# Block-sparse attention with a low-rank mixer: scores of two heads on the row halves of TensorE, a 0/1 mask product, and a searched instruction order

## The chip, the cores and the metric

One core of one Trainium2 chip. The metric is the device time of one execution in microseconds (us), the median of several runs. Every run has a state (fast or slow). Engines are called by the names in the profile: PE is TensorE's matmul row, PEld its weight loads, DVE is VectorE, ACT is ScalarE, POOL is GpSimd, and SPq is the queue of SyncE, which asks for most of the transfers (DMA: copies between the chip's memory and the core's tiles). In the profile's lines `est<-ps` means that tile est is written from tile ps; the tiles qld, kld and vld are where loads of queries, keys and values land.

## The reference, cut to what matters

Four batches, eight heads, 768 positions, 64 channels per head. Attention with a mask of 24 x 24 blocks of 32 positions: a window, the first and last block row and column, and three sampled blocks per row. Then a mixer: u = x + low-rank product over positions, and u + relu(u W1) W2 with 512 and 2048 channels.

```python
scores = scale * np.matmul(q, k.transpose(0, 1, 3, 2))        # 768 x 768 per head
scores = np.where(mask, scores, -1000000000.0)                # mask from sampled_blocks
attn = np.exp(scores - max) ; attn = attn / sum
x = np.matmul(attn, v)                                        # heads side by side: (4, 768, 512)
h = x.transpose(0, 2, 1) @ U @ V                              # rank 32
u = x + h.transpose(0, 2, 1)
out = u + np.maximum(u @ w_ch1, 0.0) @ w_ch2                  # 512 -> 2048 -> 512
```

## The kernel before: the parts that the argument touches

The work goes by pairs of heads: 16 pairs, four per batch (pair 0 to 3 are batch 0). The mask is in the scores themselves. Queries and keys lie in a tile with 64 data rows and 24 more rows of the 128 (block numbers as one-hot, and a bias of 0 or -240), so that one 128-row matmul gives score plus bias, and exp makes the masked entries vanish.

```python
def scores(i, h, g):                       # pair i, head h, block of 128 keys g
    qT, kT = augs[i]                       # 64 data rows + 24 mask rows
    psc = pscp.tile([P, 2, 512], FP32, tag="psc", name="psc")     # two PSUM banks
    for c in range(2):
        nc.tensor.matmul(psc[:, c, 0:HS], kT[:, h, g * P : (g + 1) * P],
                         qT[:, h, c * HS : (c + 1) * HS], start=True, stop=True)   # 384 columns
    nc.scalar.activation(out=est[:, g]..., in_=psc[:, :, 0:HS], func=AF.Exp, scale=0.125)
...
def av(self, h, g):                        # value product: 6 matmuls of 65 columns
...
def w1(jj, c):                             # first MLP product: 4 matmuls of 384 columns, then a ReLU
def w2(sc, part):                          # second MLP product: 4 matmuls of 512 columns
...
if i + 2 < NPAIR:
    with behind:
        last = load_qk(i + 2)              # SyncE: queries, keys
        load_v(i + 2)                      # SyncE: values
    with tc.issue_after(last.ins):
        if i == 0: load_w1((0, 1))
        elif i == 1: load_w1((2, 3))
        elif i == 4: load_w2((0, 4))       # half of the second product's weights
        elif i == 5: load_w2((8, 12))      # the other half
```

The kernel uses PSUM, where TensorE writes its results, as eight banks of 512 float32 columns. Here pools hand them out as they come free: four for scores, one for the value product, three for the rest.

The softmax here doesn't subtract the row's maximum and nothing guards it: scores larger than these inputs give would overflow.

Of the kernel before, what the change touches and what calls it, by code (L numbers as in the profile page):

```python
# [16 lines left out]
P = 128  # L17
# [3 lines left out]
def kernel(  # L21
# [29 lines left out]
    NST = 2  # L51
# [14 lines left out]
    oh_np = np.zeros((P, T, D), dtype=np.float16)  # L66
    oh_np[cols % P, cols // P, blk] = 1.0

# [11 lines left out]
    oh_dr = nc.inline_tensor(oh_np, name="onehot_const")  # L80
# [6 lines left out]
    epool = ctx.enter_context(tc.tile_pool(name="epool", bufs=2))  # L87
    xpool = ctx.enter_context(tc.tile_pool(name="xpool", bufs=2))
    upool = ctx.enter_context(tc.tile_pool(name="upool", bufs=2))
    tpool = ctx.enter_context(tc.tile_pool(name="tpool", bufs=18))  # L90
# [3 lines left out]
    pscp = ctx.enter_context(  # L94
        tc.tile_pool(name="pscp", bufs=2, space=bass.MemoryType.PSUM)
    )
    psvp = ctx.enter_context(
        tc.tile_pool(name="psvp", bufs=1, space=bass.MemoryType.PSUM)
    )
    psmp = ctx.enter_context(  # L100
        tc.tile_pool(name="psmp", bufs=3, space=bass.MemoryType.PSUM)
    )

    def psm(shape, dtype):
        return psmp.tile(shape, dtype, tag="pm", name="pm")

    id16 = consts.tile([P, P], FP16)
    oh = consts.tile([P, T, D], FP16)
# [6 lines left out]
    qst = [consts.tile([P, 2, T, P], FP16, name=f"qst{i}") for i in range(NST)]  # L115


# [4 lines left out]
    kst = [consts.tile([P, 2, T, P], FP16, name=f"kst{i}") for i in range(NST)]  # L122
# [7 lines left out]
    def load_qk(i):  # L130
        b, hp = divmod(i, HP)
        last = None
        for src, st, nm in ((q, qst, "qld"), (k, kst, "kld")):
            ld = ldpool.tile([P, 2, T, D], FP32, tag="ld" + nm, name=nm)
            nc.sync.dma_start(
                out=ld,
                in_=src[b, 2 * hp : 2 * hp + 2].rearrange("h (p t) d -> p h t d", t=T),
            )
            if i < NPE:
                sts[i, nm] = stpool.tile([P, T, 2, D], FP16, tag="st" + nm, name="st" + nm)  # L140
                dst = sts[i, nm].rearrange("p t h d -> p h t d")
            else:
                dst = st[i % NST][:, :, :, 0:D]
            last = nc.gpsimd.tensor_copy(out=dst, in_=ld)  # L144
        return last
# [45 lines left out]
    def first_turn(h, n, c):  # L191

        if n == 1:
            pt = psm([P, HS], FP32)
        elif c == 0:
            pt = pw[:, 1, 0:HS]
        else:
            pt = pscp.tile([P, 2, 512], FP32, tag="psc", name="psc")[:, 0, 0:HS]
# [9 lines left out]
    with tc.manual_schedule(  # L208
# [5 lines left out]
        pw = pscp.tile([P, 2, 512], FP32, tag="psc", name="psc")  # L214
# [7 lines left out]
        pks = [psvp.tile([P, HS], FP32, tag="pv", name="pv"), psm([P, HS], FP32)]  # L222
# [78 lines left out]
    def mask_columns():  # L301
        def both(ap):
            return ap[:, None].broadcast_to([P, 2, T, D])

        nc.sync.dma_start(out=oh, in_=oh_dr.ap())
        pb = psm([P, T, D], FP32)
        for t in range(T):
            nc.tensor.matmul(
                pb[:, t, :], ohT[:, t * P : (t + 1) * P], bias[0:NB, 0],
                start=True, stop=True,  # L310
            )
        nc.vector.tensor_copy(out=kst[0][:, 0, :, D:], in_=pb)
        nc.gpsimd.tensor_copy(out=kst[0][:, 1, :, D:], in_=kst[0][:, 0, :, D:])
        for i in range(NST):
            nc.gpsimd.tensor_copy(out=qst[i][:, :, :, D:], in_=both(oh))
            if i > 0:
                nc.gpsimd.tensor_copy(out=kst[i][:, :, :, D:], in_=kst[0][:, :, :, D:])

# [28 lines left out]

    def front(i):
        augs[i] = (qres[i % 2], kres[i % 2])
        for st, aug in zip((qst, kst), augs[i]):  # L350
            last = nc.sync.dma_start_transpose(
                aug.rearrange("d h (t p) -> d (h t) p", t=T),
                st[i % NST].rearrange("p h t d -> p (h t d)"),
            )
        return last
# [21 lines left out]
    ests = {}  # L377

    def scores(i, h, g):
        qT, kT = augs[i]  # L380
        if g == 0:
            ests[h] = epool.tile([P, T, S], FP16, tag="est", name="est")
        est = ests[h]
        psc = pscp.tile([P, 2, 512], FP32, tag="psc", name="psc")
        for c in range(2):
            nc.tensor.matmul(  # L386
                psc[:, c, 0:HS],
# [5 lines left out]
            out=est[:, g].rearrange("k (c n) -> k c n", c=2), in_=psc[:, :, 0:HS],  # L393
            func=AF.Exp, scale=0.125,
        )
        return est

    class Batch:
        def __init__(self):
            self.xf = xpool.tile([P, T, HD], FP32, tag="xf", name="xf", bufs=3)  # L400
# [5 lines left out]
            self.tT = []  # L406


    class Pair:
        def __init__(self, i, bt):  # L410
            self.b, self.hp = divmod(i, HP)
            self.bt = bt
            self.ests = {}
            self.pu = {}
            self.xh = xpool.tile([P, T, P], FP16, tag="xh", name="xh", bufs=3)
            self.ch = slice(self.hp * P, (self.hp + 1) * P)
            self.xbar = NPE <= i < NPAIR - 1

        def av(self, h, g):

            head = 2 * self.hp + h
            if g == 0:
                self.pav = psvp.tile([P, T, D + 1], FP32, tag="pv", name="pv")
            pav, est = self.pav, self.ests[h]
            for sc in range(T):
                nc.tensor.matmul(  # L426
                    pav[:, sc, :],
                    est[:, g, sc * P : (sc + 1) * P],
                    vts[self.b % 2][:, head, g, 0 : D + 1],
                    start=(g == 0 and sc == 0), stop=(g == T - 1),  # L430
                    skip_group_check=True,
                )
            if g == T - 1:
                rcp = misc.tile([P, T], FP32, tag="rcp", name="rcp")
                nc.vector.reciprocal(out=rcp, in_=pav[:, :, D])  # L435
                for dst in (
                    self.xh[:, :, h * D : (h + 1) * D],
                    self.bt.xf[:, :, head * D : (head + 1) * D],
                ):
                    self.last = nc.vector.tensor_tensor(  # L440
                        out=dst, in0=pav[:, :, 0:D],
                        in1=rcp[:, :, None].broadcast_to([P, T, D]), op=ALU.mult,
                    )

        def mix(self):
            pa = psm([P, P], FP32)
# [5 lines left out]
            nc.vector.tensor_copy(out=self.bt.a16[:, self.ch], in_=pa)  # L452


        def ut_x(self, c):
            pu = self.pu[c] = psm([P, HS], FP32)
            for j in range(3):
                nc.tensor.matmul(
                    pu[:, j * P : (j + 1) * P], self.xh[:, 3 * c + j, :], id16,
# [3 lines left out]
        def ut_a(self, c):  # L463
# [6 lines left out]
            nc.vector.tensor_copy(  # L470
                out=self.bt.uT[self.hp][:, c * HS : (c + 1) * HS], in_=self.pu[c]
            )


        def add(self, c):
            if c == 0:
                self.u16 = xpool.tile([P, T, P], FP16, tag="u16", name="u16")
            pu = psm([P, 3, P], FP32)
# [7 lines left out]
            nc.vector.tensor_add(out=self.u16[:, ts, :], in0=self.xh[:, ts, :], in1=pu)  # L486
            nc.vector.tensor_add(out=xf, in0=xf, in1=pu)  # L487
            if c == 1 and self.xbar:
                nc.sync.dma_start_transpose(
                    self.bt.uT[self.hp].rearrange("c (t p) -> c t p", t=T),  # L490
                    self.u16.rearrange("p t c -> p (t c)"),
                )

        def turn(self):
            pt = psm([P, S], FP16)
# [4 lines left out]
            nc.vector.tensor_copy(out=self.bt.uT[self.hp], in_=pt)  # L500


    def mlp_steps(b, bt):
        def w1(jj, c):
            if c == 0:
                bt.tT.append(tpool.tile([P, S], FP16, tag="tT", name="tT"))
            pt = psm([P, HS], FP32)
            for cc in range(NCC):
                nc.tensor.matmul(  # L509
                    pt,  # L510
                    w1t[:, cc, jj * P : (jj + 1) * P],
                    bt.uT[cc][:, c * HS : (c + 1) * HS],
                    start=(cc == 0), stop=(cc == NCC - 1),
                )
            dst = bt.tT[jj][:, c * HS : (c + 1) * HS]
            if c == 0:
# [4 lines left out]
        hold = {}  # L521

        def w2(sc, part):
            if part == 0:
                hold[sc] = psm([P, HD], FP32)
                if b == 0:
                    nc.tensor.matmul(  # L527
                        hold[sc], Vt[:, sc, :], bt.a16, start=True, stop=False
                    )
            for jj in range(4 * part, 4 * part + 4):  # L530
                nc.tensor.matmul(  # L531
                    hold[sc],
                    bt.tT[jj][:, sc * P : (sc + 1) * P],
                    w2t[:, jj, :],
                    start=(b > 0 and jj == 0), stop=(jj == NJJ - 1),
                )
            if part == 3:
                of = opool.tile([P, HD], FP32, tag="of", name="of")
                nc.vector.tensor_add(out=of, in0=bt.xf[:, sc, :], in1=hold[sc])  # L539
# [4 lines left out]
        def last_half(c):  # L544
# [184 lines left out]
```

## Time and profile before

| | before |
|---|---|
| time, median (runs made beside the changed kernel) | 298.88 us |
| span of the profiled run | 296.7 us |
| first to last matmul start | 292.1 us |
| of that, explained by the columns streamed | 284.2 us |
| unexplained, first 20 us / later | 4.7 / 3.3 us |

The page of the profile: busy time of an engine with its share of the span, the busy share in 40 slices as tenths, the granted TensorE clock as tenths, and the chain of work that ended last.

```profile
PE 291.4 (98%) x2775; PEld 182.3 (61%) x2775; DVE 142.0 (48%) x299; ACT 179.8 (61%) x261; POOL 50.2 (17%) x70
PE   8999999999999999999999999999999999999995
PEclk9999999999999999999999999999999999999999
...
PE 87%; ACT 12%; issue 0%; DVE 0%
...
L392 ACT ACTIVATE est<-psc 128x768 f16<-128x768 f32 x192 | 149.6, 812 | 51.6 <-PE psc L386 50.7
L386 PE MATMUL psc<-qres,kres 128*128 128x384 f16 x384 | 93.5, 325 | 1.0 <-ACT est L392 0.7
```

A group's line ends with its busy time, the mean ns of one, and its engine's idle time before it. The 325 ns of a matmul is its recorded length, and such records overlap. What counts in a stream is the time from one start to the next, and the trace gives that too: 162.8 ns behind 384 columns, 215.8 ns behind 512 and 109.2 ns behind 256. That agrees with the formula of the Trainium skill, "TensorE: Matmul & The Clock Gate", section "Back-to-back issue gap": columns divided by 2.4 plus 2.5 ns. The section calls this the gap of an isolated matmul, though, and says that a sustained stream takes some 131 ns for 512 columns; this trace has 215.8 ns in the stream, so I go by the formula. The 65-column value products start some 30 ns apart. I call a start-to-start time *explained* as far as this formula goes (at least 29.5 ns). The rest is *unexplained*: a wait, a slow clock, or a change of row tiling. The sums of explained and unexplained time in this document are worked out in this way from the matmul starts in the trace.

So from 60 us on TensorE is a full stream, and a column less is time less. Before about 41 us, exps of batch 0 on ScalarE set the pace.

One more reading matters. Six small matmuls at 32.5 us use 24 rows of the array, and the others 128. From the timeline (start, time in us, engine, line, and "xN" merged):

```profile
32.04 0.48 PE L386 MATMUL psc<-qres,kres 128*128 128x384 f16 x2
32.46 0.34 PE L308 MATMUL pm<-bias,small 24*128 24x64 f16 x6
32.74 0.35 PE L426 MATMUL pv<-vt,est 128*128 128x65 f16 x6
```

The second score matmul started at 32.204 us and streams for 163 ns; the first of 24 rows starts only at 32.459, 92 ns late. The way back costs 92 ns again.

### The profile page before, as it was taken

Reading aid. Unit: us, or ns where it says so; the run is one execution under the profiler, and the core shown is the slowest. Engines: PE = TensorE matmul, PEld = TensorE weight load, DVE = VectorE, ACT = ScalarE, POOL = GpSimd, SP = SyncE. Lnnn points to the kernel's source line nnn. Section 1 sums busy time; section 2 is a strip of 40 time slices with the busy share of each in tenths; the row PEclk is TensorE's granted clock in tenths of the full one; section 3 lists DMA queues with packets and bytes.
Section 4 is the critical chain, followed back from the end, with each engine's and each line's share of the span. In section 5 each row is a group of like instructions: output and inputs, shape, how many; then the busy total and the mean of one; then the engine's idle time right before and its main releaser. Section 6 shows DMA issues by size and latency. Waiting matters only on the chain.

```text
span 296.7 us, 6622 instructions
## 1 busy us (share of the span) xinstructions
PE 291.4 (98%) x2775; PEld 182.3 (61%) x2775; DVE 142.0 (48%) x299; ACT 179.8 (61%) x261; POOL 50.2 (17%) x70
## 2 busy tenths in 40 slices
PE   8999999999999999999999999999999999999995
PEld 3677776666666555666665556666665655565444
DVE  7766776346452525454452624346462535443112
ACT  5999997587766655767775555777875530332000
POOL 4773184014031212030201203030000000000000
PEclk9999999999999999999999999999999999999999
DMA  6899949096959494744719385662510121000111
GB/s 192 288 315 235 295 154 144 8 254 94 170 187 231 136 225 139 163 139 72 224 29 240 121 178 198 141 188 43 92 29 35 39 62 73 36 0 2 71 71 71
DMA packets 58661, 39.94 MB, mean 135 GB/s; under 512 B 40152, under 2 KB 55144, under 8 KB 58632
## 3 DMA queue, kind: packets, MB, share of 16 engines
q1 hardware_dynamic: 55764, 35.19, 43.9%
q0 software_dynamic: 2688, 4.19, 8.3%
q8 instruction: 21, 0.34, 0.5%
q10 hardware_dynamic: 180, 0.15, 0.1%
q14 instruction: 8, 0.07, 0.1%
HBM read 27.72 MB, written 6.29 MB: 115 GB/s over the span
## 4 chain that ended last, share of the span: by engine, by line
PE 87%; ACT 12%; issue 0%; DVE 0%
PE pm L509 28%; PE pm L531 27%; PE psc L386 16%; ACT est L392 12%; PE pv L426 9%; PE pm L448 1%; PE psc L218 1%; PE pm L481 1%; PE pm L550 1%; PE pm L527 0%; PE pm L497 0%; PE pm L364 0%; PE pm L201 0%; PE psc L201 0%; DVE of L555 0%
## 5 line engine op out<-in xcount | busy, mean ns | idle before, releaser
L392 ACT ACTIVATE est<-psc 128x768 f16<-128x768 f32 x192 | 149.6, 812 | 51.6 <-PE psc L386 50.7
L509 PE MATMUL pm<-uT,w1t 128*128 128x384 f16 x512 | 94.6, 326 | 0.0
L386 PE MATMUL psc<-qres,kres 128*128 128x384 f16 x384 | 93.5, 325 | 1.0 <-ACT est L392 0.7
L531 PE MATMUL pm<-w2t,tT 128*128 128x512 f16 x368 | 90.7, 379 | 0.0
L509 PEld LDWEIGHTS <-w1t 128*128 128x128 f16 x512 | 47.1, 98 | 27.0 <-issue 0.2
L426 PEld LDWEIGHTS <-est 128*128 128x128 f16 x1152 | 51.9, 97 | 16.5
L519 DVE TENSOR_SCALAR tT<-pm 128x384 f16<-128x384 f32 x64 | 35.6, 556 | 51.3 <-PE pm L509 48.6
L426 PE MATMUL pv<-vt,est 128*128 128x65 f16 x1152 | 55.7, 193 | 0.0
L517 ACT ACTIVATE tT<-pm 128x384 f16<-128x384 f32 x64 | 31.4, 490 | 38.2 <-PE pm L509 25.5
L386 PEld LDWEIGHTS <-kres 128*128 128x128 f16 x384 | 36.0, 97 | 27.0 <-issue 1.9
L531 PEld LDWEIGHTS <-tT 128*128 128x128 f16 x368 | 33.3, 98 | 30.1
L144 POOL CAST qst<-qld 128x768 f16<-128x768 f32 x10 | 8.3, 827 | 120.5 <-DMA qld<-in_q_dram 120.5
L539 DVE TENSOR_TENSOR of<-xf,pm 128x512 f32<-128x512 f32 x23 | 15.7, 684 | 25.9 <-PE pm L531 25.9
L435 DVE RECIPROCAL rcp<-pv 128x6 f32<-128x6 f32 x32 | 6.1, 192 | 38.1 <-PE pv L426 38.1
L440 DVE TENSOR_TENSOR xh<-pv,rcp 128x384 f16<-128x384 f32 x32 | 17.8, 557 | 1.0
L486 DVE TENSOR_TENSOR u<-xh,pm 128x384 f16<-128x384 f16 x24 | 13.2, 551 | 9.8 <-PE pm L481 9.3
L440 DVE TENSOR_TENSOR xf<-pv,rcp 128x384 f32<-128x384 f32 x32 | 17.5, 547 | 0.0
L154 POOL CAST vt<-vld 128x768 f16<-128x768 f32 x16 | 13.3, 828 | 14.7 <-DMA vld<-in_v_dram 14.2
L487 DVE TENSOR_TENSOR xf<-xf,pm 128x384 f32<-128x384 f32 x24 | 13.1, 547 | 0.0
L452 DVE CAST a<-pm 128x128 f16<-128x128 f32 x16 | 4.7, 291 | 15.9 <-PE pm L448 15.8
L144 POOL CAST kst<-kld 128x768 f16<-128x768 f32 x10 | 8.3, 827 | 5.1 <-DMA kld<-in_k_dram 5.1
L448 PE MATMUL pm<-xh,Ut 128*128 128x128 f16 x96 | 8.0, 219 | 0.0
(75 smaller groups left out, 111.2 us busy)
## 6 DMA issues: line engine op xcount, KB each, us to landing
vld<-in_v_dram SPq DMA_DIRECT2D x16, 384.0 KB, 5.3
out_dram<-of SPq DMA_DIRECT2D x23, 256.0 KB, 2.0
qld<-in_q_dram SPq DMA_DIRECT2D x15, 384.0 KB, 4.6
kld<-in_k_dram SPq DMA_DIRECT2D x15, 384.0 KB, 5.0
w1t<-in_moe_w_ch_dram POOLq DMA_DIRECT2D x4, 512.0 KB, 10.6
w2t<-in_moe_w_ch_dram POOLq DMA_DIRECT2D x4, 512.0 KB, 6.3
qld<-in_q_dram SPq DMA_DIRECT2D x2, 192.0 KB, 3.3
kld<-in_k_dram SPq DMA_DIRECT2D x2, 192.0 KB, 3.3
```

Source lines behind the costliest of these rows:

```text
L144: last = nc.gpsimd.tensor_copy(out=dst, in_=ld)
L154: nc.gpsimd.tensor_copy(out=vts[b % 2][:, 2 * hp : 2 * hp + 2, :, 0:D], in_=ld)
L386: nc.tensor.matmul(psc[:, c, 0:HS], kT[:, h, g * P : (g + 1) * P], qT[:, h, c * HS : (c + 1) * HS], start=True, stop=True,)
L392: nc.scalar.activation(out=est[:, g].rearrange("k (c n) -> k c n", c=2), in_=psc[:, :, 0:HS], func=AF.Exp, scale=0.125,)
L426: nc.tensor.matmul(pav[:, sc, :], est[:, g, sc * P : (sc + 1) * P], vts[self.b % 2][:, head, g, 0 : D + 1], start=(g == 0 and sc == 0), st ...
L440: self.last = nc.vector.tensor_tensor(out=dst, in0=pav[:, :, 0:D], in1=rcp[:, :, None].broadcast_to([P, T, D]), op=ALU.mult,)
L486: nc.vector.tensor_add(out=self.u16[:, ts, :], in0=self.xh[:, ts, :], in1=pu)
L509: nc.tensor.matmul(pt, w1t[:, cc, jj * P : (jj + 1) * P], bt.uT[cc][:, c * HS : (c + 1) * HS], start=(cc == 0), stop=(cc == NCC - 1),)
L517: nc.scalar.activation(out=dst, in_=pt, func=AF.Relu)
L519: nc.vector.tensor_scalar_max(out=dst, in0=pt, scalar1=0.0)
L531: nc.tensor.matmul(hold[sc], bt.tT[jj][:, sc * P : (sc + 1) * P], w2t[:, jj, :], start=(b > 0 and jj == 0), stop=(jj == NJJ - 1),)
L539: nc.vector.tensor_add(out=of, in0=bt.xf[:, sc, :], in1=hold[sc])
```

## The change

Intent: in the scores of batches 1 to 3 only 64 of the 128 rows carry data, so two heads can run at once, head 0 on rows 0 to 63 and head 1 on rows 64 to 127. The mask rows no longer fit. The mask becomes a 0/1 tile, multiplied onto the exps by VectorE. The order of TensorE, VectorE and ScalarE and the PSUM bank of each product come from a list found by a search.

```diff
-    pscp = ctx.enter_context(tc.tile_pool(name="pscp", bufs=2, space=bass.MemoryType.PSUM))
-    psvp, psmp = ...                                   # (cut)
+    PS = psum.tile([P, 8, 512], FP32, name="ps")       # all eight banks; the list names the bank
...
+    PLAN = """
+    S e S K7 e K2 k S k A A e S v R7 e S t M2 e S m R6 e S t A5 A e S A A e S X7 A e S A A6 e S
+    ...                                                # 848 entries, cut
+    p Q D6 e e W d W p W V6 p f Q v V7 e e U6 v p U5 a U3 a p U7 a U6 a Q a M6 e e U7 m U6 b p
+    """                # Q double step, H half step, e exp, p mask product, U W MLP, a b ReLU on ACT/DVE
...
+    def half_quad(i, j, hs):                           # key blocks 2j, 2j+1 of the heads hs
+        for h in hs:
+            units[h] = PS[:, 3 * h : 3 * h + 3, :].rearrange("p b n -> p (b n)")   # 3 banks a head
+        for u, lo, hi in ((0, 0, 512), (0, 512, S), (1, 0, 256), (1, 256, S)):
+            g = 2 * j + u
+            for h in hs:
+                nc.tensor.matmul(units[h][:, u * S + lo : u * S + hi],
+                    kT[drows[h], g * P : (g + 1) * P], qT[drows[h], lo:hi], ...)   # 64 rows
+        for h in hs:
+            exp of 128x1536 on ScalarE; then
+            nc.vector.tensor_mul(out=both[h], in0=both[h], in1=mask[:, 2 * j : 2 * j + 2, :])
...
+    def mask_tile():                                   # in batch 0, once
+        for r in range(16):
+            for d in range(3):
+                ts = [t for t in range(T) if (6 * r + t) // BLK == d]
+                if ts:
+                    nc.sync.dma_start(out=mask[r : P : 16, ts[0] : ts[-1] + 1, :],
+                        in_=table[8 * d : 8 * d + 8, None, :].broadcast_to([8, len(ts), S]))
```

There are 34 double steps and 4 half steps. The mask tile takes 18 transfers on SyncE.

## The prediction

> **What bounds the kernel.** TensorE's stream of columns. In the trace a matmul starts after the one before it by a time that grows with the columns of the one before: 162.8 ns for 384 columns, 215.8 ns for 512, some 30 ns for the 65-column value product. Summed over all matmuls these times make 284.2 of the 292.1 us from first to last matmul; of the 7.9 us left, 4.7 lie in the first 20 us and 1.8 in the next 20. From 60 us on TensorE loses 0.1 us in each 20. The chain of waits agrees: PE 87%, ACT 12% (exps of batch 0, to about 41 us). After that VectorE (48% busy) and ScalarE (61%) have slack.
>
> **What it removes.** Scores of pairs 4 to 15 are now 64 rows deep. They were 288 matmuls of 384 columns (46.8 us). Now 34 double steps have four matmuls per head (512, 256, 256, 512 columns), the heads on opposite row halves. Side by side, a step streams 650 ns plus some 30 ns offset instead of 1300: 23.1 us for 34. Four half steps have one head alone and gain nothing (2.6 us). Saved: about 21 us. The skill page "TensorE: Matmul & The Clock Gate", Part 3, says matmuls on different row groups run concurrently; nothing in this trace shows it yet.
>
> **What it adds.**
> - Changing the row tiling drains the array ("TensorEngine Tiling (Array Packing)", Key Properties). The trace agrees: around the six 24-row matmuls at 32.5 us the stream stops 92 ns on entry and 92 on leaving. 38 steps times two: 7 us.
> - VectorE: 72 mask products of 128x1536 f16. The trace has no such form. My estimate is 0.9 us each at two elements per cycle (65 us in all), 1.7 us at one. ReLUs move away: 64 to 39 on VectorE (556 ns each, -14 us), 64 to 89 on ScalarE (490 ns). VectorE then has about 145 us of work in the 235 us after batch 0.
> - ScalarE: 72 exps of 1536 columns for 144 of 768 (702 ns start to start); estimated 1.34 us each.
> - PSUM: a double step holds six of eight banks until two exps, 2.7 us, are over. Meanwhile the MLP has two banks and what comes free. There new stalls of TensorE can arise; the order was searched to avoid them. I allow 2 us.
> - DMA: 1.2 MB of mask rows while the first pairs load, half as much transposing later. Off the path.
>
> **The sum.** 298.95 - 21 + 7 + 2 - 2 (some of the early waits) = 285 us. All of it counts, because TensorE's stream is the path. Batch 0, to about 45 us, should hardly change.
>
> Prediction: 284.5 us, range 277 to 293. Chances: faster by over 2% 0.84, within 2% 0.11, slower 0.05.
>
> **What would show each step.** In the timeline the heads' score matmuls start some 30 ns apart, and a step takes about 0.7 us. The gaps before and after a step are about 90 ns longer than the columns explain. Mask products last 0.9 us. TensorE's unexplained time after 60 us sums to about 7 us plus stalls. ScalarE and VectorE stay under 75% busy; the chain stays mostly PE.
>
> **What would make it wrong.** No concurrency of the halves (then about 306 us). Weight loads of a half that aren't hidden behind its own matmul (some 60 ns each, 10 us in all). Mask products at one element per cycle: VectorE would hold back value products and MLP banks, several us. A cheaper drain: down to 279. PSUM stalls above 2 us.

## The result, and the profile after

The changed kernel takes 332.44 us (332.27 to 333.10, four runs) against 298.88 us: **11.2% slower**, ratio 1.112, 95% interval 1.110 to 1.114. Ratios in this document are the mean time of one kernel's fast runs over that of the other's of the same rounds, so not quite the ratio of the medians that are quoted.

The same parts of the page, changed kernel (L568 is the first MLP product, L722 the row-half scores, L731 their exps, L737 the mask product):

```profile
PE 285.3 (86%) x2759; PEld 166.3 (50%) x2759; DVE 192.7 (58%) x342; ACT 182.0 (55%) x214; POOL 51.1 (15%) x66
PE   6899904996689889898789999988979899999995
PEclk9999965999599999999999999999999999999999
...
PE 57%; DMA 16%; ACT 13%; SPq 6%; issue 5%; POOL 2%; DVE 1%; POOLq 0%; ACTq 0%
...
L731 ACT ACTIVATE est<-ps 128x1536 f16<-128x1536 f32 x72 | 100.7, 1448 | 48.1 <-PE ps L722 47.3
L737 DVE TENSOR_TENSOR est<-est,mask 128x1536 f16<-128x1536 f16 x72 | 72.0, 1002 | 22.5 <-ACT est L731 22.5
L722 PE MATMUL ps<-qpl,kpl 64*128 64x512 f16 (+1 forms) x288 | 31.9, 328 | 0.0
```

PE has holes now: the sixth and seventh slice (41 to 58 us), the tenth and eleventh (74 to 91 us), with the clock down to 5 or 6 tenths in three of these, and many slices at 8. Only 57% of the chain is PE now, where it was 87%; transfers, exps and SyncE's queue have 35%. VectorE, at 58%, is not crowded.

The row halves themselves did what they should. These are the starts (ns from the first) of the eight score matmuls of the double step at 138.86 us, with their columns:

```
0 (512)   3 (512)   226 (256)   230 (256)   336 (256)   339 (256)   445 (512)   448 (512)
```

Two heads start 3 ns apart and a step streams 664 ns (median of 34), where two heads one after the other would take about 1300.

Who waited for whom on TensorE (us in total, times, longest), changed kernel:

```profile
PE ps L568 <- ACT est L731: 13.1, 15, 1.1
PE ps L672 <- POOL stqld L149: 12.6, 1, 12.6
PE ps L595 <- DMA w2t<-in_moe_w_ch_dram: 6.1, 2, 4.3
PE ps L500 <- ACT est L731: 3.7, 4, 1.0
PE ps L288 <- DVE kres L240: 1.6, 1, 1.6
PE ps L568 <- DMA uT<-u: 1.5, 1, 1.5
PE ps L534 <- ACT est L731: 0.8, 1, 0.8
```

The balance of TensorE from first to last matmul start, in us. "Stop" is an unexplained time over 0.45 us. The last column is the best kernel of the experiments, further down:

| | before | changed | e7 |
|---|---|---|---|
| columns | 284.2 | 262.1 | 263.8 |
| changes between row tilings | 0.2 | 7.1 | 8.0 |
| unexplained, first 20 us | 4.7 | 6.5 | 5.3 |
| stops after 20 us | 0 | 41.9 | 2.6 |
| the rest (small waits, slow clock) | 3.1 | 8.4 | 4.2 |
| first to last matmul | 292.1 | 326.1 | 283.9 |

The columns fell by 22.1 us and the changes of tiling cost 7.1: as predicted. The 41.9 us of stops were not. They are of four kinds:

1. **12.8 us at 41.5 us**: TensorE wants to turn the queries of pair 5, and they have not arrived. Timelines of SyncE's queue and of GpSimd, first before:

```profile
20.75 0.37 SPq L135 DMA_DIRECT2D qld<-in_q_dram  x1
```

and in the changed kernel:

```profile
19.82 28.26 SPq L664 DMA_DIRECT2D mask<-table  x18
48.18 1.35 SPq L144 DMA_DIRECT2D qld<-in_q_dram  x1
...
53.61 0.83 POOL L149 CAST stqld<-qld 128x768 f16<-128x768 f32 x1 [17.47 <-DMA qld<-in_q_dram]
```

The 18 mask transfers take SyncE's queue from 19.8 to 48.2 us. The queries of pair 5, asked for at 20.75 us before, are asked for at 48.18 us, and GpSimd casts them at 53.6. The queue's own waits say that part of the 28 us is waiting for earlier transfers:

```profile
SPq L664 <- DMA kld<-in_k_dram: 5.1, 1, 5.1
SPq L664 <- DMA qld<-in_q_dram: 3.3, 1, 3.3
SPq L664 <- DMA vld<-in_v_dram: 2.5, 1, 2.5
```

   Each issue in the trace carries one of eight semaphores in turn. From the third mask issue on, an issue also waits on that semaphore, which the transfer eight before it had used. The quickest issues take 0.60 us, others 1.44 us, one 1.60 us (16.7 us for all 18; the rest of the 28 us is nearly all waiting); why, these runs don't settle.

2. **4.5 and 2.1 us at 79.5 and 85.4 us**: the second half of the weights of the second MLP product has not landed. Its two transfers land at 84.11 and 87.70 us, and TensorE goes on at 84.15 and 87.74.

3. **20.9 us in 20 stops of 0.6 to 1.3 us**: a product placed after a double step waits for the step's second exp. One of them, timelines of TensorE and ScalarE (L595 is the second MLP product, L500 the mixer):

```profile
133.70 0.82 PE L722 MATMUL ps<-qpl,kpl 64*128 64x512 f16 x8
134.45 1.04 PE L595 MATMUL ps<-w2t,tT 128*128 128x512 f16 x4
135.33 0.38 PE L588 MATMUL ps<-a,Vt 128*128 128x512 f16 x1
135.54 1.03 PE L595 MATMUL ps<-w2t,tT 128*128 128x512 f16 x4
137.40 0.49 PE L500 MATMUL ps<-xh,Ut 128*128 128x128 f16 x6 [0.83 <-ACT est L731]
...
134.56 2.79 ACT L731 ACTIVATE est<-ps 128x1536 f16<-128x1536 f32 x2 [1.37 <-PE ps L722]
```

   The two exps end at 137.35 us. L500 is written into bank 5, which the second of them was reading (the list says "M5"), and starts at 137.40.

4. **1.7 us at 149.7 us** for a transposed u.

After a long stop the clock is low, too. From the view by stretches (span of the stretch, busy times, granted clock, DMA share, GB/s), changed kernel:

```profile
41.00:60.00 19.00, 6.34 (x74) 4.67 (x72) 4.09 (x11) 3.72 (x5) 4.08 (x6) 0.64 0.63 155
79.00:92.00 13.00, 6.95 (x54) 3.74 (x54) 3.73 (x7) 2.79 (x2) 1.70 (x3) 0.61 0.62 101
```

"TensorE: Matmul & The Clock Gate", Part 1, says that TensorE's clock falls to half after an idle window of about 3.4 us and comes back after a busy one. The trace agrees in part. Behind the 4.5 us stop 512-column matmuls start 427 ns apart instead of 216, and the two stretches of half clock last 13.65 and 10.24 us, four and three times 3.41. But the clock fell already 2.7 and 2.3 us into the two longest stops, before 3.4 us of idling had passed.

### The profile page after: what moved, and what is told of

Same layout as the page of the kernel before. It is cut to its first block, busy times and chain, and to the rows that moved or that the text cites. A ratio compares the mean times of both kernels' runs of the same rounds, so it can differ in the third digit from the quotient of the medians.

```text
span 330.5 us, 6605 instructions
## 1 busy us (share of the span) xinstructions
PE 285.3 (86%) x2759; PEld 166.3 (50%) x2759; DVE 192.7 (58%) x342; ACT 182.0 (55%) x214; POOL 51.1 (15%) x66
## 4 chain that ended last, share of the span: by engine, by line
PE 57%; DMA 16%; ACT 13%; SPq 6%; issue 5%; POOL 2%; DVE 1%; POOLq 0%; ACTq 0%
PE ps L568 22%; PE ps L595 18%; ACT est L731 13%; PE ps L722 8%; DMA vld<-in_v_dram 8%; PE ps L406 5%; SPq L664 4%; DMA w2t<-in_moe_w_ch_dram 2%; DMA uT<-u 2%; DMA qld<-in_q_dram 2%; PE ps L500 1%; DMA vld<-in_moe_V_dram 1%; PE ps L534 1%; DMA kld<-in_k_dram 1%; PE ps L615 1%
## 5 line engine op out<-in xcount | busy, mean ns | idle before, releaser
L731 ACT ACTIVATE est<-ps 128x1536 f16<-128x1536 f32 x72 | 100.7, 1448 | 48.1 <-PE ps L722 47.3
L568 PE MATMUL ps<-uT,w1t 128*128 128x384 f16 x512 | 95.7, 326 | 14.7 <-ACT est L731 13.1
L595 PE MATMUL ps<-w2t,tT 128*128 128x512 f16 x368 | 91.0, 384 | 6.1 <-DMA w2t<-in_moe_w_ch_dram 6.1
L737 DVE TENSOR_TENSOR est<-est,mask 128x1536 f16<-128x1536 f16 x72 | 72.0, 1002 | 22.5 <-ACT est L731 22.5
L578 ACT ACTIVATE tT<-ps 128x384 f16<-128x384 f32 x89 | 43.7, 491 | 70.4 <-PE ps L568 69.4
L568 PEld LDWEIGHTS <-w1t 128*128 128x128 f16 x512 | 47.9, 97 | 52.1 <-issue 22.5
L595 PEld LDWEIGHTS <-tT 128*128 128x128 f16 x368 | 34.9, 99 | 44.8 <-issue 11.0
L406 PE MATMUL ps<-vt,est 128*128 128x65 f16 x1152 | 45.3, 196 | 0.0
L580 DVE TENSOR_SCALAR tT<-ps 128x384 f16<-128x384 f32 x39 | 21.6, 555 | 29.6 <-PE ps L568 29.3
L706 ACT ACTIVATE est<-ps 128x768 f16<-128x768 f32 x36 | 26.2, 810 | 13.3 <-PE ps L697 13.3
L722 PE MATMUL ps<-qpl,kpl 64*128 64x512 f16 (+1 forms) x288 | 31.9, 328 | 0.0
L603 DVE TENSOR_TENSOR of<-xf,ps 128x512 f32<-128x512 f32 x23 | 15.7, 683 | 27.3 <-PE ps L595 27.3
L722 PEld LDWEIGHTS <-kpl 64*128 64x128 f16 x288 | 11.8, 95 | 16.1 <-issue 10.7
L474 DVE TENSOR_TENSOR xh<-ps,rcp 128x384 f16<-128x384 f32 x32 | 17.8, 558 | 1.1
L161 POOL CAST vt<-vld 128x768 f16<-128x768 f32 x16 | 15.0, 936 | 11.2 <-DMA vld<-in_v_dram 10.2
L469 DVE RECIPROCAL rcp<-ps 128x6 f32<-128x6 f32 x32 | 6.2, 193 | 17.6 <-PE ps L406 17.6
```

What stands on the lines that cost most here:

```text
L406: nc.tensor.matmul(pav[:, sc, :], est[:, n, sc * P : (sc + 1) * P], vts[b % 2][:, 2 * hp + h, g, 0 : D + 1], start=(g == 0 and sc == 0), s ...
L474: self.last = nc.vector.tensor_tensor(out=dst, in0=pav[:, :, 0:D], in1=rcp[:, :, None].broadcast_to([P, T, D]), op=ALU.mult,)
L568: nc.tensor.matmul(pt, w1t[:, cc, jj * P : (jj + 1) * P], bts[b].uT[cc][:, c * HS : (c + 1) * HS], start=(cc == 0), stop=(cc == NCC - 1),)
L578: nc.scalar.activation(out=dst, in_=pt, func=AF.Relu)
L580: nc.vector.tensor_scalar_max(out=dst, in0=pt, scalar1=0.0)
L595: nc.tensor.matmul(po, tts[b, c, jj][:, s * P : (s + 1) * P], w2t[:, jj, :], start=(b > 0 and jj == 0), stop=(jj == NJJ - 1), skip_group_c ...
```

## The experiments

Theories after the result. **A**: the 18 mask transfers hold up SyncE's queue, and late queries and late weights follow. **C**: after a double step the list uses banks 3 to 5 first, the very ones that come free last. Rivals: **B**, VectorE with 72 more operations holds things back; the transfers' bytes, not their place in the queue; and that the row halves are worth nothing. Times are medians of four runs; before measured 299.1 to 299.3 us beside them. In e3 and e12, where one run of four is slow, the table has the median of the three fast ones.

| run | time, us | ratio to before |
|---|---|---|
| changed kernel | 332.44 | 1.112 |
| e1 mask by matmul | 320.43 | 1.070 |
| e2 mask transfers later in the queue | 329.23 | 1.101 |
| e3 no mask product (wrong result) | 333.34 | 1.115 |
| e4 banks swapped | 312.65 | 1.046 |
| e5 = e1 + e4 | 301.13 | 1.006 |
| e6 = e5 + weights asked for earlier | 292.41 | 0.976 |
| e7 = e6 + other banks at the start | 290.51 | 0.971 |
| e8 = e7, heads in turn | 290.38 | 0.971 |
| e10 = e7, last u of a batch turned on TensorE | 291.44 | 0.973 |
| e11 = e7, both heads on one row half | 311.38 | 1.039 |
| e12 = changed, both heads on one row half | 347.27 | 1.165 |
| e13 = e7, no mask product (wrong result) | 288.89 | 0.965 |

(The slow runs are 338.96 us in e3 and 352.31 us in e12; with them the medians are 334.15 and 348.90 us. The fast runs are 332.37 to 334.95 and 346.76 to 350.54 us.)

**e1: the mask made by matmul.** For each block of keys, 24-row matmuls of the mask rows that batch 0 has anyway, compared on VectorE; 12 of each, spread over batch 0 in the list. No mask transfer is left.

```diff
-    mask_tile()                                    # 18 transfers
+    def mask_part(t, c, n):
+        nc.tensor.matmul(pm, kres[0][rows, 0, t * P : (t + 1) * P],
+                         qres[0][rows, 0, c * HS : (c + 1) * HS], start=True, stop=True)
+        nc.vector.tensor_single_scalar(out=mask[:, t, c * HS : (c + 1) * HS], in_=pm,
+                                       scalar=-1.0, op=ALU.is_ge)
```

> Changed kernel, but the 0/1 mask is made by 12 matmuls of 24 rows and 12 VectorE comparisons in batch 0, and the 18 mask transfers are gone. Theory A (the transfers hold up SyncE's queue from 19.8 to 48.2 us, so queries and keys of pairs 4 and 5, and through them the weights of the second MLP product, come late): the 12.8 us stop of TensorE at 41.5 us and the stops of 4.5 and 2.1 us near 79 to 88 us vanish with their half clock, 20 to 25 us in all: 307 to 313 us. The stops of about 1 us after the double steps stay. Rival (VectorE's mask products or the order alone make the loss): less than 5 us.

Measured: 320.43 us, 12 faster, not 20 to 25. The stop at 41.5 us is gone; its query load is asked for at 20.89 us. The stops for the weights are still there, only earlier (4.3 us at 68.2 us, 1.8 at 73.9). So theory A is right for the first stop and wrong for the second: the weights are late for another reason (e6). The 20 stops behind the steps stay as they were (13.1, 3.7 and 0.8 us of waits for exps, the same three numbers).

**e2: the same transfers behind the loads of pair 5.** (The text says ahead of pair 4 for the place in the changed kernel. In fact pair 4's loads are through by 19.8 us, and it is pair 5's that stood behind.)

```diff
-            if c == 1:
-                mask_tile()
...
+        if i == 3:
+            mask_tile()                            # after loads(3), which asks for pair 5
```

> Changed kernel, same 18 mask transfers, but put into SyncE's queue behind the loads of pair 5 instead of ahead of those of pair 4. Theory A1 (it is the place in the queue): the stop at 41.5 us shrinks from 12.8 to under 3 us, though the first mask products may wait a little for late mask rows: 308 to 318 us. Rival A2 (it is the 1.2 MB that takes bandwidth from the loads): the loads of pairs 4 and 5 are late all the same and the time stays above 326 us.

Measured: 329.23 us, only 3 faster. By the time alone the rival A2 (above 326 us) would have won, and A1's 308 to 318 us is missed. The trace decides between them: the stop at 41.5 us is gone, as A1 says, with the same bytes in another place. Pair 5's queries are asked for at 21.14 us and cast by GpSimd at 41.56 us, not at 53.61. But the transfers take 28.9 us again, from 23.6 to 52.6 us. Timelines of VectorE and TensorE (here L735 is the mask product, L523 a copy that the first product needs, L720 the scores):

```profile
57.20 0.96 DVE L735 TENSOR_TENSOR est<-est,mask 128x1536 f16<-128x1536 f16 x1 [9.20 <-DMA qld<-in_q_dram]
58.07 0.55 DVE L523 CAST uT<-ps 128x384 f16<-128x384 f32 x1
...
58.68 1.04 PE L720 MATMUL ps<-qpl,kpl 64*128 64x256 f16 x6 [8.63 <-DVE uT L523]
```

The first mask product stands at the head of VectorE's queue for 9.2 us (the view names the load that landed last; I take it to be mask rows that it waits for, as they are its only new input), the copy behind it waits, and TensorE stops 8.6 us there instead of 12.8 us earlier. So the cost is a queue held for 28 us, and moving it only chooses who pays.

**e3: without the mask products.** Its output is wrong, which doesn't matter for the time.

```diff
-                then("p", lambda: nc.vector.tensor_mul(out=both[h], in0=both[h], in1=mask[...]))
+                then("p", lambda: None)
```

> Changed kernel without the 72 mask products (wrong result on purpose). Rival B (VectorE, with 72 us more work, holds back the value products and the banks): 10 us or more faster, under 322 us, and the 1 us stops after the double steps vanish. Theory (the stops after a double step wait for the second exp on ScalarE, not for VectorE): under 5 us faster, and some 20 stops of about 1 us remain.

Measured: 333.34 us, no faster. Rival B falls: 72 us of VectorE work are worth nothing here.

**e4: banks swapped.** In a double step the first head gets banks 3 to 5, the second 0 to 2. The list, and so what waits for bank 3, 4 or 5, is unchanged.

```diff
-            units[h] = PS[:, 3 * h : 3 * h + 3, :].rearrange("p b n -> p (b n)")
+            first = 3 * (1 - h) if len(hs) == 2 else 3 * h
+            units[h] = PS[:, first : first + 3, :].rearrange("p b n -> p (b n)")
```

> Changed kernel, but in a double step the first head has banks 3 to 5 and the second banks 0 to 2; order of everything else the same. Theory C (after a double step the order uses banks 3, 4 and 5 first, which only the second exp, 2.8 us later, sets free): now the first exp frees them 1.34 us sooner, so most of the 20 stops of about 1 us vanish: 12 to 20 us faster, 312 to 320 us; the stops at 41.5 and near 80 us stay. Rival (the stops come from VectorE, or from late weights): within 4 us of the changed kernel.

Measured: 312.65 us, 19.8 faster; theory C holds. Of 24 stops five are left: the query (12.3 us at 43.1 us), the weights (5.7 and 1.1), the transposed u (2.2) and a new one of 0.7 us. The place shown above, in e4:

```profile
127.83 0.82 PE L723 MATMUL ps<-qpl,kpl 64*128 64x512 f16 x8
128.59 1.04 PE L595 MATMUL ps<-w2t,tT 128*128 128x512 f16 x4
129.46 0.38 PE L588 MATMUL ps<-a,Vt 128*128 128x512 f16 x1
129.68 1.03 PE L595 MATMUL ps<-w2t,tT 128*128 128x512 f16 x4
130.54 0.50 PE L500 MATMUL ps<-xh,Ut 128*128 128x128 f16 x6
...
128.69 2.79 ACT L732 ACTIVATE est<-ps 128x1536 f16<-128x1536 f32 x2 [1.37 <-PE ps L723]
```

L500 starts right behind the product before it, 0.9 us before the second exp ends.

**e5: e1 and e4 together.**

> Mask by matmul (e1) and swapped banks (e4) together. e1 took 12 us and e4 20 us off the changed kernel. If the two causes are separate, the sum is 32 us: 299 to 303 us, level with the kernel before. If they share the loss (a stop only moves), less: above 306 us. The stop near 68 us, for the second half of the second product's weights, should still be there, about 4 to 6 us with a slow clock behind it.

Measured: 301.13 us. The two gains add up (12.0 and 19.8; together 31.3 us): two separate causes, and together they bring the kernel back to level.

**e6: all weights of the second product asked for at pair 4.** First, why they were late: when GpSimd asks for the second half (the first of its two transfers, from GpSimd's timeline), in the kernel before:

```profile
68.32 0.74 POOL L338 DMA_DIRECT2D w2t<-in_moe_w_ch_dram  x1
```

and in e1:

```profile
66.79 0.74 POOL L325 DMA_DIRECT2D w2t<-in_moe_w_ch_dram  x1
```

Nearly the same time. But before, the second product starts at 80.8 us and first reads these weights at 84.2 us, when they have lain there since 74.0. The new list reaches them at 68.2 us, and in e1 they land at 72.6.

```diff
                 elif i == 4:
-                    load_w2((0, 4))
-                elif i == 5:
-                    load_w2((8, 12))
+                    load_w2((0, 4, 8, 12))
```

> e5 with all four loads of the second product's weights asked for at pair 4, not two at pair 4 and two at pair 5. Theory: the faster scores bring the second product forward, before the weights asked for at pair 5 are there; the stops near 68 and 74 us and their half clock vanish, 6 to 9 us faster than e5: 291 to 296 us. Rival: the stop there waits for the first product's banks; no change.

Measured: 292.41 us, 8.7 faster, as expected. The wait for the weights (6.4 us in e5) is gone from TensorE's waits, and with it its half clock. This kernel is faster than the one before, by 2.4%.

**e7: other banks at the start.** The changed kernel replaced a pool by a fixed ring of banks, so that an early transpose got a bank that VectorE still had to read.

```diff
-        return bank((7, 2, 5)[ring["psm"] % 3], shape, dtype)
+        return bank((2, 5, 7, 5, 7, 2, 5)[ring["psm"] - 1], shape, dtype)
```

> e6 with other PSUM banks for the seven small products at the start, so that the first transposes of the queries don't wait for VectorE to read the mask rows (1.6 us on TensorE at 7 us, 1.6 us on ScalarE behind it). Theory: batch 0 is held by ScalarE, so its delay is passed on: 1.5 to 2.5 us faster than e6, 289 to 293 us. Rival: the slack of batch 0 swallows it, under 0.5 us.

Measured: 290.51 us, 1.9 faster. The wait "L286 for DVE L238" of 1.6 us (L288 for L240 in the changed kernel) is gone. **e7 beats both kernels: 2.9% faster than before (ratio 0.9706, interval 0.9676 to 0.9736) and correct.** Its page:

```profile
PE 280.4 (97%) x2769; PEld 163.8 (57%) x2769; DVE 193.8 (67%) x351; ACT 181.0 (63%) x214; POOL 51.4 (18%) x66
PE   8999999999999999899999999999999999999995
...
PE 84%; ACT 7%; DMA 4%; DVE 3%; issue 1%; ACTq 0%; DVEq 0%
```

**e8: the heads' matmuls in turn.** In the instruction list all four of head 0, then all four of head 1.

```diff
-        for u, lo, hi in (...):
-            for h in hs:
+        for h in hs:
+            for u, lo, hi in (...):
                 nc.tensor.matmul(...)
```

> e7, but in a double step the four matmuls of the first head come before the four of the second, so that they can't run side by side (row halves, banks, products and order else the same). Theory: a step streams 1300 instead of 661 ns, and with the stops gone TensorE pays for nearly all of it: 34 times 0.64 us is 22 us, less a few us because the first exp starts earlier: 15 to 22 us slower than e7. Rival (the row halves are worth nothing here because exps set the pace): under 5 us slower.

Measured: 290.38 us, no difference, which reads like the rival. But the trace shows that the experiment did not do what it should. The compiled list has, in a step, columns 512, 256, 256, 512, 512, 256, 256, 512, the first four on rows 0 to 63 and the last four on rows 64 to 127. The starts in the trace come, in 33 of the 34 double steps, in the order 512, 512, 256, 256, 256, 256, 512, 512, with the second 13 ns after the first, and a step takes 674 ns. The trace doesn't name the row half of a matmul, but this order fits only one reading: TensorE ran the head on the other row half ahead of its place in the list. So e8 could not settle what the halves are worth; it takes a shared half.

**e11: both heads on rows 0 to 63.** The second head's scores are computed from the first's rows, wrong on purpose. (The comparison with the reference still passes: with inputs this small the scores hardly move the exps. So passing is no proof of right scores.)

```diff
-                    kT[drows[h], g * P : (g + 1) * P],
-                    qT[drows[h], lo:hi],
+                    kT[drows[0], g * P : (g + 1) * P],
+                    qT[drows[0], lo:hi],
```

> e7 with the second head's scores computed from rows 0 to 63 too (wrong result on purpose), so that both heads of a double step need the same row half and can't run side by side, whatever order TensorE takes them in. Theory (side by side is what saved the time, and with the stops gone TensorE's stream is the path): steps of 1300 instead of 661 ns, 34 times 0.64 us = 22 us; 15 to 22 us slower than e7: 305 to 312 us. Rival (the exps set the pace, the halves are worth little): under 5 us slower.

Measured: 311.38 us, 20.9 slower than e7. A step now takes 1311 ns (median) instead of 664, which over 34 steps is 22.0 us. So the row halves earn nearly all of their stream time once nothing else stops TensorE.

**e12: the same in the changed kernel.**

> The changed kernel, unmended, with both heads on rows 0 to 63 (wrong result on purpose). Theory: there TensorE waits about 1 us after some 20 steps for the second exp; a longer step eats into that wait, so the gain of the row halves was largely handed back: only 5 to 12 us slower than the changed kernel, 337 to 344 us. Rival (waits and stream are separate, nothing was handed back): 20 us or more slower.

Measured: 347.27 us, some 15 slower (14.8 by the medians of fast runs). I had expected 5 to 12: that longer steps would be swallowed by the waits behind them. The waits for exps did shrink, but only from 17.6 to 13.4 us in total. So even in the unmended kernel the row halves paid out about two thirds of their worth (14.8 of 22.0 us), and the 11% were lost beside them.

**e10: the last u of batch 1 turned on TensorE.** In e7 the first product of batch 1 waits 2.2 us at 121 us for a transposing transfer.

```diff
-                if c == 1 and self.i < NPAIR - 1:
+                if c == 1 and self.i not in (2 * HP - 1, NPAIR - 1):
...
-    p Q D6 e e W d W p W V6 p f Q v ...
+    p Q D6 e e W d W p W T5 z V6 p f Q v ...
```

> e7, with the last u of batch 1 turned by six TensorE transposes and one VectorE copy instead of a transposing transfer. In e7 the first product of batch 1 waits 2.2 us at 121 us for that transfer, which stood in SyncE's queue behind an output and a load. Theory: the wait goes, 0.3 us of transposes come: 1 to 2 us faster than e7, 288 to 289.5 us. Rival: the wait moves to another transfer of the same batch; within 0.5 us of e7.

Measured: 291.44 us, not faster. That wait is gone, but the new copy stands ahead of other work of VectorE, and a value product waits 0.9 us there. The trace has also 1.8 us of waiting for the queries at 43 us, where nothing was changed. Inconclusive within 1 us; not kept.

**e13: e7 without the mask products.** The edit of e3.

> e7 without the 72 mask products (wrong result on purpose). Theory: with the stops mended TensorE's stream is still the path and VectorE has slack at 67%; under 2 us faster than e7. Rival: VectorE's 70 us of products now hold something back; 4 us or more faster.

Measured: 288.89 us, 1.6 faster. VectorE's 70 us of products are almost wholly off the path in the mended kernel as well.

## Why the prediction was wrong

The prediction was 284.5 us, range 277 to 293; measured 332.44. Two of its steps failed: the 2 us allowed for new stalls behind the exps, which came to 20.9 us, and the mask transfers taken to be off the path, which cost 12.8 us of TensorE. Two smaller losses, the late weights and a bank at the start, were not in it at all. Point by point:

- *TensorE's stream of columns bounds the kernel*: right for the kernel before. For the changed kernel it no longer was: PE 87% of the chain became 57%.
- *Saved: about 21 us*: right. Columns fell by 22.1 us; a step streams 664 ns (predicted 680). Undoing it costs 20.9 us in e11.
- *Changing the row tiling costs 92 ns, 38 steps times two, 7 us*: right, 76 changes cost 7.1 us.
- *Mask products last 0.9 us, VectorE has slack*: right. The median is 0.957 us. The 0.9 was an estimate at two results per cycle, which "VectorE: DVE Perf Modes", "Mode 2×_1P", gives for 16-bit data; e3 and e13 show that they cost 0 and 1.6 us.
- *Two exps, 2.7 us, hold six of eight banks; I allow 2 us for new stalls*: the mechanism was named, and its size was wrong by a factor of ten: 20.9 us of stops. The failing thought was "the order was searched to avoid them". Behind 24 of the 34 steps the list sent the first product that needed a bank of the step to banks 3 to 5, which the second exp frees (behind the other ten no product needed one before the next step). All 20 stops lie behind those 24. This could have been read blind: the list names the banks, U5, U3, M5 behind "e e", and between stand two to four products, mostly of 0.65 or 0.86 us, against 2.7 us of exps. Swapping the banks gave back 19.8 us (e4).
- *DMA: 1.2 MB of mask rows, off the path*: this step failed. I counted bytes. What mattered was 18 issues in an in-order queue with the loads of the next pairs behind them: 28 us of SyncE, 12.8 us of TensorE, and slow clock behind it (12.0 us, e1).
- *Not in the prediction at all*: the weights of the second product, asked for at the same place, are needed sooner when the list moves that product forward (8.7 us, e6); and the fixed ring of banks at the start (1.9 us, e7). "Batch 0 should hardly change" was wrong for that reason.
- *The sum*: the four mends take 12.0, 19.3, 8.7 and 1.9 us off in this order of building (e1, e5, e6, e7), together 41.9 us, from 332.4 to 290.5. What remains above my sum can be read from e7's balance: its unexplained time (first 20 us, stops, the rest) is 12.1 us where my sum had 7.8, because the early waits didn't shrink and small waits grew; changes of tiling take 8.0 us for 7.2, as the matmul-made mask adds ten. That comparison is worked out, and no run isolates its parts.

What stays open: why the search chose banks 3 to 5 behind a step, and why some mask issues take 0.60 us and others 1.44 us.

## What to carry to other kernels

A saving on the busiest engine is a forecast only for the case that its inputs come as early as its new pace needs them: go through every transfer queue in program order and ask what now stands ahead of what, and when the first reader wants it. Count transfers by issues and by queue, not by bytes. Where an order is fixed by hand or by a search, check for each shared buffer (here a PSUM bank) that the first product written into it comes later than the last read of it; the bank numbers were worth 20 us here, about as much as the row halves themselves.

## What the Trainium skill lacked or had wrong

- "TensorE: Matmul & The Clock Gate", section "Back-to-back issue gap", has some 131 ns for 512 columns in a sustained stream. Here it is 215.8 ns, as its formula for an isolated matmul gives.
- The same page, Part 1, asks for about 3.4 us of idling before the clock falls. Here it fell 2.7 and 2.3 us into two long stops.
- The same page, Part 3, says matmuls are "strict FIFO, no reordering" in start and end, and Part 2 that they stay in program order. In e8, with four matmuls on one row half ahead of four on the other in the list, the starts alternate in 33 of 34 steps (13 ns apart, 674 ns a step instead of about 1311). As far as the trace's start times go, order holds within a row half, not between halves. A semaphore that relies on the last matmul in the list ending last should be thought over where row halves differ.
- The same page's about 4 ns between tiles on different row groups agrees: 3 ns.
- "TensorEngine Tiling (Array Packing)", Key Properties, says that a change of tiling mode drains TensorE, without a figure. Here it is 92 to 96 ns each way between 128 rows and 24 or 64 rows, on top of the columns (76 changes, 7.1 us).
- "Perfetto Trace Analysis", "DMA Instruction — HWDGE (DVE, Sync)", says that the sequencer which issues a transfer waits for its semaphores and is free for the next instruction only at the end of the issue. No page that I found gives the time of an issue, or warns of the loads behind it. Here 18 transfers took SyncE's queue 28.3 us, 0.60 to 1.60 us an issue plus waits for semaphores used eight transfers earlier.
- "VectorE: DVE Perf Modes", Mode 2×_1P, held for an f16 product in place: 957 ns for 1536 elements, where the f32 sum from PSUM in the output (L603) takes some 680 ns for 512.
